# Background matmuls in four column tiles, a lead-in that walks both head pairs by key chunk, and Q of the last two query chunks made later

## The chip, the cores and the metric

The kernel runs on one core of one Trainium2 chip. The metric is the device time of one execution in microseconds (us), taken from runs of the changed kernel and of the kernel before that alternate on the same chip. The time before was 1268.96 us (median of 3 runs). All comparisons are between fast runs.

The engines are called as in the profile. PE is TensorE (PEld its weight loads), DVE is VectorE, ACT is ScalarE, POOL is GpSimd, SP issues the DMAs. "L593" is line 593 of the kernel that the view belongs to.

## The reference

One pre-LN transformer block in bf16, with sequence 2048, width 1024, 32 heads of 32, and an FFN of width 3584.

```python
def _A_ref(x, wqkv, wo):                       # attention, no mask
    q, k, v = split(x @ wqkv)                  # H = 32 heads, Dh = 32
    p = softmax(einsum("bhqd,bhkd->bhqk", q, k) * Dh ** -0.5)
    return merge(einsum("bhqk,bhkd->bhqd", p, v)) @ wo
def _B_ref(x, w1, b1, w2, b2):
    return gelu(x @ w1 + b1) @ w2 + b2         # tanh form
h  = x + _A_ref(_layernorm(x), wqkv, wo)
h2 = h + _B_ref(_layernorm(h), w1, b1, w2, b2)
```

## The kernel before

The kernel states every operation as a task with an estimated cost. A list scheduler written in Python then fixes the instruction order of each engine before the kernel is built. On the chip each engine is given its list in that order and waits on semaphores.

The 2048 queries are four chunks of 512. Attention goes over chunks, then over 16 head pairs, then over 16 key tiles, so there are 1024 exponentials of 128x1024 on ACT, 256 to a chunk. "qk" matmuls use the PE array in four row tiles, "pv" matmuls (with the softmax sum) in four column tiles. Four such matmuls, one for each tile, are issued as a pack. Everything else on the PE is "background" (bg): the Q, K and V projections while chunk 0 runs, and the output projection Wo, the second layer norm's transposes and the FFN of chunk n-1 while chunk n runs. Background has one PSUM bank (7), pv has one (6), qk has six.

```python
def proj(which, g, tc, bank, evac, direct=False):      # Q or K of head group g (two pairs), 512 tokens
    for dc in range(DC):
        pe(lambda p, dc=dc: p.matmul(psum[:, bank, :], Wall[:, blk, dc, c:c + P], xnT[:, tc, dc, :], ...),
           MM, ...)                                     # mode="full" by default
    ...                                                 # copy to stg; K: 4 copies into KT2; Q: to DRAM
def layer_norm(x_ap, B_x, o_ap, B_o, prio):             # one tile of 128 tokens
    ...                                                 # DVE: statistics; POOL: 7 tiny steps
    dve(lambda v: v.tensor_scalar(o_ap, x_ap, mvr[:, i, :], rden[:, i, :], ALU.subtract, ALU.mult), ...)
...
for tc in range(4):                                     # the lead-in: one key chunk after another
    for t4 in range(4):
        ...; ln_tile(tt, xslot[tt], 0)
        tr_tile(tt, xslot[tt], lb(), "act")             # 8 transposes, copied out by ACT
    proj(1, 0, tc, lb(), "act")
    ...
    attention_round(0, 0, 2 * tc)                       # pair 0 only
    for t4 in range(4): proj_v(4 * tc + t4, 0, lb(), "act")
    attention_round(0, 0, 2 * tc + 1)
def rest_of_projections():
    for g in range(1, G):
        for tc in range(4): proj(1, g, tc, 7, "dve")
        proj(0, g, 0, 7, "dve")
        ...                                             # V of the other 512 columns while g is 1..3
    for tc in range(1, 4):                              # Q of chunks 1, 2, 3
        for g in range(G): proj(0, g, tc, 7, "dve")
...
for qc in range(1, NCH):
    wo_ln2(R1, qc - 1, [7]); ffn1(R1, qc - 1, [7]); ffn2(R1, qc - 1, [7])
    attention_chunk(qc); attention_flush()
```

When a head pair is done, `finish` copies the pv bank to `Osb` and `Dsb`. After every second pair it takes reciprocals and writes `OT[g]`. `Osb`, `Dsb` and `OT` exist once: `OT[g]` can't be written while Wo of the previous chunk still reads it, and until it is written the next pair can't empty the pv bank.

The softmax here doesn't subtract the row's maximum and nothing guards it: scores larger than these inputs give would overflow.

## Time and profile before

| stretch | what | measured |
|---|---|---|
| 0 to 29 us | x, layer norm, first K, Q | first exponential at 29.2 |
| 29 to 331 | chunk 0, with all of K, Q, V | 302 us for 256 exponentials |
| 332 to 1119 | chunks 1, 2, 3 | 261, 262, 262 us |
| 1119 to 1267.5 | tail: Wo, layer norm, FFN of chunk 3, full-width matmuls | 149 us |

Exponentials were counted in the trace's records. A chunk goes from the start of its first to the start of its last exponential. Without any wait a head pair of 16 takes 14.8 us, and 256 exponentials take 237 us.

The page's first part gives busy time, share of the span and instructions by engine:

```profile
PE 1156.2 (91%) x9099; PEld 377.0 (30%) x9248; DVE 676.7 (53%) x1148; ACT 1052.7 (83%) x1174; POOL 67.3 (5%) x236
```

The stretches view has, per stretch, busy us and (instructions) of PE, PEld, DVE, ACT, POOL, then clock, DMA share and GB/s:

```profile
100.00:200.00 100.00, 92.56 (x754) 29.32 (x771) 44.29 (x94) 85.17 (x93) 0.00 (x0) 1.00 0.10 30
...
500.00:600.00 100.00, 92.20 (x782) 24.21 (x794) 27.39 (x38) 97.85 (x103) 0.00 (x0) 1.00 0.17 56
```

ACT is nearly full from about 300 us on, and the PE is at 92% beside it. In the first 300 us ACT has room. The timeline of ACT (start us, duration us, instruction, count, and in brackets the wait before it) shows one whole gap:

```profile
76.25 15.49 ACT L593 ACTIVATE PT<-ps 128x1024 bf16<-128x1024 f32 x16
102.52 27.82 ACT L593 ACTIVATE PT<-ps 128x1024 bf16<-128x1024 f32 x30 [10.77 <-PE ps L583]
```

The timeline of the PE in a steady round shows what fills the PE (L719 background, L583 qk, L603 one half of a pv pack; the other half, L607, is left out):

```profile
602.00 0.39 PE L603 MATMUL ps<-PT,V 128*32 128x512 bf16 x2
...
602.23 0.38 PE L603 MATMUL ps<-PT,V 128*32 128x512 bf16 x2
...
602.55 0.39 PE L719 MATMUL ps<-a_w2r,gT 128*128 128x512 bf16 x1
...
602.87 0.40 PE L583 MATMUL ps<-QT_67,KT_65 32*128 32x512 bf16 x4
...
603.20 0.82 PE L719 MATMUL ps<-a_w2r,gT 128*128 128x512 bf16 x3
...
603.95 0.39 PE L603 MATMUL ps<-PT,V 128*32 128x512 bf16 x2
```

Read the starts: two pv packs are 0.23 us apart, but pv to background takes 0.32, background to qk 0.32, and qk to background 0.33. Each change of array mode adds about 0.1 us. The trace has 1731 changes.

### The profile page before, as it was taken

To read this page: it belongs to the slowest core of one execution; us is meant where nothing else is said; L and a number is where in the kernel's file an instruction comes from. 1 tells how busy PE (TensorE), PEld (TensorE's weight loads), DVE (VectorE), ACT (ScalarE), POOL (GpSimd) and SP (SyncE) were. 2 spreads that over 40 slices of the span, in tenths; PEclk is the share of its full clock that TensorE was granted. 3 is DMA by queue.
4 is the path that set the end of the run, shared out by engine and by line. 5 is a ranking of instruction groups with operands and counts; after the bars stand their busy time and mean duration, and the time that the engine had idled before them with its cause. 6 is when DMAs were issued, how large, how long until landed. Compare 5 with 4: busy or idle time off the path is not lost.

```text
span 1267.5 us, 21571 instructions
## 1 busy us (share of the span) xinstructions
PE 1156.2 (91%) x9099; PEld 377.0 (30%) x9248; DVE 676.7 (53%) x1148; ACT 1052.7 (83%) x1174; POOL 67.3 (5%) x236
## 2 busy tenths in 40 slices
PE   5999998999998999999989999999899999996989
PEld 2432222233322232222232332222323322233434
DVE  4534446543447886222368882222689832237971
ACT  3777877999999999999999999999999999930220
POOL 5500000000011000000020000000200000002000
PEclk9999999999999999999999999999999999997989
DMA  5740020021132322040523320404433303041404
GB/s 141 167 116 13 13 76 17 26 88 47 43 92 80 87 81 63 18 133 18 168 75 88 88 72 18 134 18 138 125 88 94 107 22 110 25 146 50 117 10 140
DMA packets 152098, 99.84 MB, mean 79 GB/s; under 512 B 25153, under 2 KB 149953, under 8 KB 152002
## 3 DMA queue, kind: packets, MB, share of 16 engines
q1 hardware_dynamic: 152002, 98.47, 26.7%
q8 instruction: 72, 1.18, 0.4%
q14 instruction: 24, 0.20, 0.0%
HBM read 89.92 MB, written 8.26 MB: 77 GB/s over the span
## 4 chain that ended last, share of the span: by engine, by line
PE 67%; DVE 20%; ACT 5%; issue 4%; POOL 3%; DMA 1%; SPq 0%; POOLq 0%; DVEq 0%
PE ps L719 16%; PE ps L603 16%; PE ps L583 10%; PE ps L511 9%; PE ps L685 8%; ACT PT L593 4%; PE ps L660 3%; PE ps L552 3%; DVE a_xh L690 3%; DVE gT L698 2%; DVE Osb L617 2%; DVE Dsb L621 2%; DVE a_uu L694 2%; DVE Dsb L615 2%; DVE st L461 1%
## 5 line engine op out<-in xcount | busy, mean ns | idle before, releaser
L593 ACT ACTIVATE PT<-ps 128x1024 bf16<-128x1024 f32 x1024 | 969.3, 1034 | 51.6 <-PE ps L583 40.4
L603 PE MATMUL ps<-PT,V 128*32 128x512 bf16 x2048 | 312.7, 384 | 25.7 <-DVE Osb L617 21.1
L607 PE MATMUL ps<-PT,ones_50 128*32 128x512 bf16 x2048 | 312.6, 385 | 0.0
L719 PE MATMUL ps<-a_w2r,gT 128*128 128x512 bf16 x848 | 239.8, 387 | 5.4 <-issue 4.9
L583 PE MATMUL ps<-QT_67,KT_65 32*128 32x512 bf16 x2048 | 202.3, 385 | 12.4 <-ACT PT L593 8.4
L685 PE MATMUL ps<-hnT,a_w1r 128*128 128x512 bf16 x630 | 166.8, 382 | 14.1 <-DVE a_xh L690 7.1
L615 DVE COPY Dsb<-ps 64x512 f32<-64x512 f32 x64 | 44.4, 693 | 250.1 <-PE ps L607 248.2
L511 PE MATMUL ps<-xnT,Wall 128*128 128x512 bf16 x478 | 128.3, 387 | 8.0 <-DVE stg L520 3.8
L603 PEld LDWEIGHTS ps<-PT,V 128*32 128x32 bf16 x2048 | 67.6, 94 | 202.8 <-issue 148.4
L621 DVE RECIPROCAL Dsb<-Dsb 128x128 f32<-128x128 f32 x128 | 113.7, 924 | 0.5
L583 PEld LDWEIGHTS ps<-QT_67,KT_65 32*128 32x128 bf16 x2048 | 52.0, 91 | 198.6 <-ACT PT L593 149.0
L719 PEld LDWEIGHTS ps<-a_w2r,gT 128*128 128x128 bf16 x896 | 69.3, 98 | 138.4 <-issue 98.4
L520 DVE CAST stg<-ps 128x512 bf16<-128x512 f32 x59 | 40.3, 683 | 106.7 <-PE ps L511 92.6
L696 ACT ACTIVATE b_th<-b_uu 128x512 f32<-128x512 bf16 x28 | 17.6, 630 | 88.0 <-DVE b_uu L694 88.0
L685 PEld LDWEIGHTS ps<-hnT,a_w1r 128*128 128x128 bf16 x672 | 53.8, 97 | 100.1 <-issue 33.7
L690 DVE TENSOR_SCALAR a_xh<-ps,b1f 128x512 bf16<-128x512 f32 x84 | 62.2, 741 | 22.5 <-PE ps L685 20.6
L552 PE MATMUL ps<-Wall,xnT 128*128 128x512 bf16 x245 | 61.3, 381 | 9.6 <-DVE V L559 4.5
L511 PEld LDWEIGHTS ps<-xnT,Wall 128*128 128x128 bf16 x512 | 44.2, 98 | 85.6 <-issue 29.8
L607 PEld LDWEIGHTS ps<-PT,ones_50 128*32 128x32 bf16 x2048 | 67.5, 94 | 0.0
L660 PE MATMUL ps<-a_w1r,OT 128*128 128x512 bf16 x256 | 65.7, 382 | 0.1
L698 DVE SCALAR_TENSOR_TENSOR gT<-a_th,a_xh 128x512 bf16<-128x512 f32 x84 | 56.7, 675 | 16.2 <-ACT a_th L696 15.9
L464 POOL CAST mvb<-mv 128x2 bf16<-128x2 f32 x32 | 7.2, 230 | 1077.1 <-DVE mv L463 1077.1
(53 smaller groups left out, 706.7 us busy)
## 6 DMA issues: line engine op xcount, KB each, us to landing
a_w2r<-in_B_w_dram SPq DMA_DIRECT2D x56, 512.0 KB, 4.5
a_w1r<-in_B_w_dram SPq DMA_DIRECT2D x42, 512.0 KB, 3.9
a_w1r<-in_A_wo_dram SPq DMA_DIRECT2D x16, 512.0 KB, 3.8
QT_67<-q_scratch SPq DMA_DIRECT2D x62, 128.0 KB, 2.7
b_w1r<-in_B_w_dram SPq DMA_DIRECT2D x14, 512.0 KB, 3.8
Wall<-in_A_wqkv_dram SPq DMA_DIRECT2D x16, 256.0 KB, 5.2
xr<-in_A_x_dram SPq DMA_DIRECT2D x16, 256.0 KB, 2.9
a_xr_82<-in_A_x_dram SPq DMA_DIRECT2D x32, 128.0 KB, 3.3
```

The costliest lines, as they stand in the source:

```text
L511: pe(lambda p, dc=dc: p.matmul(psum[:, bank, :], Wall[:, blk, dc, c:c + P], xnT[:, tc, dc, :], start=(dc == 0), stop=(dc == DC - 1)), MM, ...
L552: pe(lambda p, dc=dc: p.matmul(psum[:, bank, :], xnT[:, tc, dc, t4 * P:(t4 + 1) * P], Wall[:, blk, dc, :], start=(dc == 0), stop=(dc == DC ...
L583: return p.matmul(psum[:, 2 * us[half] + j, :], KT2[r0:r0 + 32, p16, tc, i, :], QT2[r0:r0 + 32, qs, pr, :], start=True, stop=True, tile_po ...
L593: act(lambda a, u=u, s=s: a.activation(PT[:, s, :, :], psum[:, 2 * u:2 * u + 2, :], ACT.Exp, bias=0.0, scale=SCALE), 1024, reads=[B_ps[2 * ...
L603: fns.append(lambda p, j=j, h=h: p.matmul(psum[32 * j:32 * j + 32, 6, :], V[:, kt, 32 * h:32 * h + 32], PT[:, s, j, :], start=first, stop= ...
L607: fns.append(lambda p, j=j: p.matmul(psum[64 + 32 * j:96 + 32 * j, 6, :], ones32[:, :], PT[:, s, j, :], start=first, stop=last, tile_posit ...
L621: dve(lambda v, k=k: v.reciprocal(Dsb[:, 128 * k:128 * k + 128], Dsb[:, 128 * k:128 * k + 128]), 0.9, reads=[B_Dsb[0][k], B_Dsb[1][k]], wr ...
L660: pe(lambda p, g=g, k=k, s=s, t4=t4, bank=bank: p.matmul(psum[:, bank, :], OT[:, g, t4 * P:(t4 + 1) * P], R.w1[:, s:s + 2, g, :], start=(k ...
L685: pe(lambda p, dc=dc, s=s, f=f, bank=bank: p.matmul(psum[:, bank, :], R.w1[:, s, dc, f * P:(f + 1) * P], hnT[:, dc, :], start=(dc == 0), s ...
L690: dve(lambda v, i=i, fc=fc, bank=bank: v.tensor_scalar(R.xh[:, i, :], psum[:, bank, :], b1f[:, fc:fc + 1], None, ALU.add), c_dve_ps(512), ...
L698: dve(lambda v, i=i, fc=fc: v.scalar_tensor_tensor(gT[:, fc, :], R.th[:, i, :], 1.0, R.xh[:, i, :], ALU.add, ALU.mult), c_dve(512), reads= ...
L719: pe(lambda p, fc=fc, s=s, t4=t4, bank=bank: p.matmul(psum[:, bank, :], gT[:, fc, t4 * P:(t4 + 1) * P], R.w2[:, s, fc % 4, :], start=False ...
```

## The change

The change has three intents. Background matmuls become four column tiles of 32, so that they share pv's mode. The lead-in does both pairs of g=0 per key chunk, with only a quarter of V, so that exponentials start earlier and denser. Q of chunks 2 and 3 leaves the crowded chunk 0. One part of the second intent is easily read over: for key chunks 1 to 3 the last step of the layer norm moves from DVE to POOL, planned at 1.4 us a tile.

```diff
+    def mm(bank, lhsT, rhs, start, stop, reads, narrow, cols=(0, 512)):
...
+        if narrow:                                     # all background but the tail's
+            for j in range(4):
+                fns.append(lambda p, j=j: p.matmul(psum[32*j:32*j+32, bank, c0:c1], lhsT[:, 32*j:32*j+32], rhs,
+                           start=start, stop=stop, tile_position=(0, 32 * j), skip_group_check=True))
+            pe(fns, occ, ..., mode="col")
...
+    def layer_norm(tiles, prio, norm="dve"):           # up to four tiles share the small steps
+            eng, cost = (dve, 0.58) if norm == "dve" else (pool, 1.4)
+            eng(lambda e, ...: e.tensor_scalar(o_ap, x_ap, mvr[...], rden[...], ALU.subtract, ALU.mult), cost, ...)
...
+    def late_q(R, qc):                                 # Q of chunk qc from x kept in DRAM, weights through the FFN ring
...
     for tc in range(4):
+        ev = "act" if tc == 0 else "dve"
+        for h in ((0, 1), (2, 3)) if tc == 0 else ((0, 1, 2, 3),):
+            ln_tiles([tts[k] for k in h], 0, "dve" if tc == 0 else "pool")
...
+        for k in range(8):
+            att.qk(0, [(k % 2, 4 * tc + k // 2)])      # both pairs, one key tile each
+            if k == 1: proj_v(4 * tc, 0, lb(), ev)     # 256 columns of V, two token tiles
+            if k == 3: proj_v(4 * tc + 2, 0, lb(), ev)
...
     for qc in range(1, NCH):
+        if qc + 1 < NCH:
+            late_q(R1, qc + 1)
         wo_ln2(R1, qc - 1, [7])
```

Also changed: 20 warm-up matmuls at the start, other costs in the scheduler, one more PT buffer, and `PV_FORCE` (how many pv packs may wait before the scheduler puts them ahead of background) raised from 3 to 5.

## The prediction

> **What bounds it now.** The timeline of the scalar engine shows three stretches. (1) Lead-in and first query chunk: the first exponential starts at 29.2 us, the 256 of chunk 0 end at 331. Dense exponentials start every 0.92 us (14.8 us for one head pair of 16), so 256 need 237 us: about 65 us are lost, 10.8 us of it in one gap at 92 to 102 us, where the PE finishes K and Q of the next pair. (2) Chunks 1 to 3: 261 us each, against 254 us of scalar work (237 + 28 tanh of about 0.6). The stretches table has ACT 97 to 98% busy, PE 92 to 94%; both are nearly full. (3) A tail from the last exponential (1119 us) to the end, 148 us, PE work at full width.
>
> In a steady round of 1.95 us the timeline shows one bg matmul, qk, three bg, two pv, bg again: four changes of array mode. Starts are 216 ns apart between bg matmuls but 309 from bg to pv, 321 back, 327 after qk: each change costs about 0.1 us. I count 1731 changes, some 170 us of PE time. The Trainium skill ("TensorEngine Tiling (Array Packing)", Key Properties) says a change of tiling mode drains the array; this trace agrees, at 0.1 us.
>
> **What the change does.**
> - Background matmuls in four column tiles share pv's mode, so a round has two changes: about 700 fewer, 70 us of PE time. Packs of four pv matmuls follow each other in 216 to 227 ns, so I cost a column-tiled 512-column matmul at 0.2225 us, and a 256-column piece at 0.115, an estimate from the same spacing. It quadruples the instructions (eight per pack). No pv run here is longer than five packs, so sustained issue is unproven; the 256-column V pieces are the worst. The same page says column tiling disables Fast Weight Load; pv's four loads took 0.1 us, hidden.
> - Lead-in: 32 exponentials instead of 16, V only a quarter at first, evictions moved from ACT to DVE. Per key chunk I estimate PE 13 us, DVE 12, ACT 8, against 14.3 us now. Warm-up matmuls and earlier x loads bring the first exponential to about 26 us. But both pairs of g=0 are spent when the lead-in ends (about 74 us), and K and Q of g=1 (13.5 us on one bank, then 7 us through DRAM) are exposed: a gap of 12 to 20 us, next exponential about 94 us (102 now).
> - Chunk 0 afterwards: per g, 72 matmul-equivalents (16 us) plus attention 14 us = 30 us, against 29.6 us of ACT: balanced. It ends near 306 us: -25 us.
> - Chunks 1 and 2 get 64 matmuls of Q each: PE about 244 of 254 us. Late Q delays Wo, which holds the output tiles and so may stall pv for some us. I take 258, 257, 255: -13 us.
> - Tail: fewer POOL steps in layer norm, -2 us; with the backlog gone the PE idles 6 us before Wo. Net about 0.
>
> Sum: 1269 - 25 - 13 - 2 = 1229 us.
>
> **What would show it.** Steps between column packs near 220 ns; about 1050 changes; exponentials of pair 2 from about 94 us; chunk 0's last near 306 us; chunks 1 to 3 at 255 to 258 us; last exponential near 1080 us; tail unchanged at 146 to 149 us.
>
> **What would make it wrong.** Column packs issue-bound (over 0.25 us, V pieces over 0.15): chunk 0 stays PE-bound and the gain shrinks to 1 or 2%. A longer gap after the lead-in, or pv stalls behind Wo. On the other side, a faster lead-in, or chunk 0 wholly ACT-bound: near 1210 us.
>
> Chances: faster 0.75, same 0.21, slower 0.04. Range 1205 to 1256 us.

## The result, and the profile after

The changed kernel took 1264.05 us (median of 4 runs, 1263.26 to 1266.15) against 1269.44 (4 runs). The ratio is 0.9958, with a 95% interval of 0.994 to 0.9975. Ratios are the mean time of one kernel's fast runs over that of the other's of the same rounds, so not quite the ratio of the medians. The change gained 0.4%, where 3.2% was forecast.

| | before | after | predicted |
|---|---|---|---|
| first exponential, us | 29.2 | 25.5 | 26 |
| period of a key chunk in the lead-in, start to start | 12.9 to 14.4 | 22.8 to 23.8 | about 13 to 14 |
| first exponential of pair 2 | 102.5 | 130.3 | 94 |
| last exponential of chunk 0 | 331 | 342.6 | 306 |
| chunks 1, 2, 3 | 261, 262, 262 | 255.5, 260.6, 254.2 | 258, 257, 255 |
| start of the last exponential to the end | 149.5 | 145.8 | unchanged |
| mode changes | 1731 | 1086 | 1050 |

Page, first part, then two stretches of the lead-in and the two that answer to those shown of before:

```profile
PE 1154.2 (91%) x17266; PEld 465.2 (37%) x17276; DVE 686.6 (54%) x1186; ACT 1027.8 (81%) x1145; POOL 83.6 (7%) x108
```

```profile
40.00:60.00 20.00, 14.77 (x230) 7.47 (x230) 9.45 (x22) 7.76 (x8) 12.81 (x8) 0.76 0.14 41
60.00:80.00 20.00, 13.79 (x226) 7.29 (x222) 8.04 (x18) 6.74 (x7) 13.84 (x8) 0.76 1.06 210
100.00:200.00 100.00, 90.98 (x1798) 43.70 (x1800) 50.85 (x110) 71.86 (x77) 0.00 (x0) 0.97 0.12 35
...
500.00:600.00 100.00, 99.01 (x1608) 37.69 (x1604) 27.08 (x37) 99.70 (x109) 0.00 (x0) 1.00 0.35 102
```

From 500 to 600 us ACT is now 99.7% busy, where it was 97.9%. That is what the column tiles were for. In the two lead-in stretches shown, no engine is busy more than three quarters of the time (PE 69 to 74%, POOL 64 to 69%), and the clock is down to 0.76. The PE timeline of a steady stretch shows that the tiles themselves did what was hoped (L435 is now all narrow background; x4 is one pack):

```profile
523.63 0.38 PE L649 MATMUL ps<-PT,V 128*32 128x512 bf16 x2
...
523.84 0.82 PE L435 MATMUL ps<-a_w2r,gT 128*32 128x512 bf16 x12
524.60 0.39 PE L629 MATMUL ps<-QT_65,KT_63 32*128 32x512 bf16 x4
524.92 0.40 PE L435 MATMUL ps<-a_w2r,gT 128*32 128x512 bf16 x4
525.15 0.38 PE L649 MATMUL ps<-PT,V 128*32 128x512 bf16 x2
```

Between pv and background a start now follows after 0.21 to 0.23 us, in either direction. Over the whole trace a pack of four takes 216 ns, and a 256-column V pack 109 ns (medians). So neither the quadrupled instructions nor the weight loads cost anything that shows here.

The loss is in the lead-in. The ACT timeline shows waits between the key chunks, and then a long one:

```profile
60.63 1.02 ACT L638 ACTIVATE PT<-ps 128x1024 bf16<-128x1024 f32 x1 [0.70 <-PE ps L629]
72.05 4.69 ACT L638 ACTIVATE PT<-ps 128x1024 bf16<-128x1024 f32 x5 [10.38 <-PE ps L629]
...
95.52 7.69 ACT L638 ACTIVATE PT<-ps 128x1024 bf16<-128x1024 f32 x8 [8.28 <-PE ps L629]
...
130.34 1.94 ACT L638 ACTIVATE PT<-ps 128x1024 bf16<-128x1024 f32 x2 [27.14 <-PE ps L629]
```

The wait is put down to the qk matmuls on the PE, but the PE was itself waiting. The waits view for 20 to 103 us says for what (us in total, times, longest):

```profile
PE ps L504 <- POOL xb L498: 22.3, 12, 2.7
```

L504 are the transposes, and L498 is the last step of the layer norm, now on POOL. The POOL timeline of one key chunk, with the start of the next:

```profile
47.31 0.19 POOL L488 CAST mvb<-mv 128x8 bf16<-128x8 f32 x1 [6.76 <-DVE mv L485]
...
49.03 1.01 POOL L494 TENSOR_TENSOR rden<-denb,cexp 128x4 f32<-128x4 bf16 x1
50.21 15.07 POOL L498 TENSOR_SCALAR xb<-xrb,mvr,rden 128x1024 bf16<-128x1024 bf16 x4 [0.18 <-DVE st L483]
71.09 0.19 POOL L488 CAST mvb<-mv 128x8 bf16<-128x8 f32 x1 [5.80 <-DVE mv L485]
```

From 47.31 to 71.09 is the period of 23.8 us: 2.9 us of small steps, 15.1 us for four tiles, and 5.8 us in which POOL waits for DVE statistics. The groups view gives the mean of the same step, in ns, before and after (the number just before the second bar):

```profile
L474 DVE TENSOR_SCALAR xb<-xr,mvr,rden 128x1024 bf16<-128x1024 bf16 x16 | 8.6, 542 | 10.1 <-POOL rden L472 10.0
```

```profile
L498 POOL TENSOR_SCALAR xb<-xrb,mvr,rden 128x1024 bf16<-128x1024 bf16 x8 | 30.2, 3782 | 0.4 <-POOL rden L494 0.2 <-DVE st L483 0.2
```

The step takes 542 ns on DVE and 3782 ns on POOL, 7.0 times as long. All twelve on POOL took 3.78 to 3.79 us, whatever the DVE was doing beside them. The diff plans it at 1.4 us. The Trainium skill ("GPSIMD Engine Reference", sections 3.1 and 4.1) says that two-input elementwise work there is about two times slower than on VectorE, and one-input work about at line rate. For this step, with one tensor input and two per-partition scalars, the trace doesn't agree, and the measurement decides.

### The profile page after: what moved, and what is told of

Read it like the earlier page. It is cut to its first block, busy times and chain, and to the rows that moved or that the text cites. A ratio compares the mean times of both kernels' runs of the same rounds, so it can differ in the third digit from the quotient of the medians.

```text
span 1261.5 us, 37733 instructions
## 1 busy us (share of the span) xinstructions
PE 1154.2 (91%) x17266; PEld 465.2 (37%) x17276; DVE 686.6 (54%) x1186; ACT 1027.8 (81%) x1145; POOL 83.6 (7%) x108
## 3 DMA queue, kind: packets, MB, share of 16 engines
q1 hardware_dynamic: 162978, 106.85, 29.2%
## 4 chain that ended last, share of the span: by engine, by line
PE 57%; ACT 27%; DVE 10%; POOL 4%; issue 2%; DMA 0%; POOLq 0%; DVEq 0%
PE ps L435 30%; ACT PT L638 26%; PE ps L439 9%; PE ps L649 9%; PE ps L629 8%; POOL xb L498 4%; DVE a_xh L728 3%; DVE gT L736 1%; DVE stg L544 1%; DVE Dsb L667 1%; DVE a_uu L732 1%; PE ps L504 1%; DVE Osb L663 1%; DVE st L483 1%; DVE Dsb L661 1%
## 5 line engine op out<-in xcount | busy, mean ns | idle before, releaser
L435 PE MATMUL ps<-hnT,a_w1r 128*32 128x512 bf16 x3200 | 211.2, 382 | 14.9 <-DVE a_xh L728 13.9
L435 PE MATMUL ps<-a_w2r,gT 128*32 128x512 bf16 x2688 | 196.5, 381 | 0.0
L649 PEld LDWEIGHTS ps<-PT,V 128*32 128x32 bf16 x2048 | 96.8, 97 | 125.3 <-issue 36.0
L661 DVE COPY Dsb<-ps 64x512 f32<-64x512 f32 x64 | 44.4, 694 | 131.1 <-PE ps L653 129.8
L435 PE MATMUL ps<-xnT,Wall 128*32 128x512 bf16 x1536 | 107.4, 400 | 8.3 <-DVE stg L544 6.1
L435 PEld LDWEIGHTS ps<-hnT,a_w1r 128*32 128x32 bf16 x3200 | 72.6, 96 | 114.4 <-issue 38.5
L435 PEld LDWEIGHTS ps<-a_w2r,gT 128*32 128x32 bf16 x2688 | 68.5, 96 | 81.9 <-issue 28.3
L653 PEld LDWEIGHTS ps<-PT,ones_50 128*32 128x32 bf16 x2048 | 96.8, 97 | 0.0
L734 ACT ACTIVATE b_th<-b_uu 128x512 f32<-128x512 bf16 x28 | 17.6, 630 | 84.2 <-DVE b_uu L732 84.2
L435 PE MATMUL ps<-Wall,xnT 128*32 128x256 bf16 x2048 | 67.3, 274 | 3.3 <-DVE V L602 2.4
L758 DVE SCALAR_TENSOR_TENSOR a_ost<-ps,hch 128x512 bf16<-128x512 f32 x24 | 16.4, 684 | 97.0 <-PE ps L435 96.9
L544 DVE CAST stg<-ps 128x512 bf16<-128x512 f32 x46 | 31.2, 678 | 55.7 <-PE ps L435 55.6
L435 PEld LDWEIGHTS ps<-xnT,Wall 128*32 128x32 bf16 x1536 | 37.4, 100 | 61.7 <-issue 20.6
```

What stands on the lines that cost most here:

```text
L435: fns.append(lambda p, j=j: p.matmul(psum[32 * j:32 * j + 32, bank, c0:c1], lhsT[:, 32 * j:32 * j + 32], rhs, start=start, stop=stop, tile ...
L544: dve(lambda v: v.tensor_copy(stg[:, s, :], psum[:, bank, :]), c_dve_ps(512), reads=[B_ps[bank]], writes=[B_stg[s]])
L649: fns.append(lambda p, j=j, h=h: p.matmul(psum[32 * j:32 * j + 32, bank, :], V[:, kt, 32 * h:32 * h + 32], PT[:, s, j, :], start=first, st ...
L653: fns.append(lambda p, j=j: p.matmul(psum[64 + 32 * j:96 + 32 * j, bank, :], ones32[:, :], PT[:, s, j, :], start=first, stop=last, tile_po ...
L661: dve(lambda v: v.tensor_copy(Dsb[64 * pr:64 * pr + 64, :], psum[64:128, bank, :]), c_dve_ps(512), reads=[B_ps[bank]], writes=B_Dsb[pr], p ...
```

## The experiments

Theory A: the norm on POOL paces the lead-in. Rival B: the column packs, the V pieces or the slow clock do. Rival C: POOL's time would be hidden, were it not for a fixed order made from a wrong cost. Other theories came later, as below. Times are medians of the fast runs; the ratio is to before. The kernel before was near 1269 us.

| run | edit, on top of | time, us | ratio [95%] |
|---|---|---|---|
| e1 | norm on DVE, on after | 1240.6 | 0.9767 [0.9747, 0.9787] |
| e2 | POOL planned at 3.8 us, on after | 1251.4 | 0.9868 [0.9842, 0.9895] |
| e3 | background at full width, on after | 1303.2 | 1.026 [1.0232, 1.0288] |
| e4 | column tiles alone, on before | 1248.3 | 0.9837 [0.982, 0.9854] |
| e5 | e1 again | 1240.5 | 0.9768 [0.9745, 0.979] |
| e6 | K, Q of g=1 in the lead-in, on e1 | 1237.2 | 0.9743 [0.9719, 0.9766] |
| e7 | late Q after the first FFN part, on e1 | 1227.9 | 0.9672 [0.9649, 0.9695] |
| e8 | e6 and e7, norm on ACT | 1230.0 | 0.9688 [0.9662, 0.9714] |
| e9 | Q of g=1 before K, on e7 | 1235.1 | 0.9722 [0.9704, 0.974] |
| e10 | dummy matmuls in the tail, on e7 | 1224.9 | 0.9649 [0.9626, 0.9672] |
| e11 | no late Q, on e7 | 1243.7 | 0.9793 [0.9773, 0.9814] |
| e12 | lead-in walks one pair, on e7 | 1228.7 | 0.9671 [0.9651, 0.9692] |
| e13 | late Q moved as in e7, on after | 1265.3 | 0.9965 [0.9934, 0.9997] |
| e14 | late Q moved, on e2 | 1248.3 | 0.9825 [0.9797, 0.9852] |
| e15 | e7 again | 1230.4 | 0.9686 [0.966, 0.9712] |
| e16 | e10 again | 1225.5 | 0.9646 [0.9621, 0.9671] |

All sixteen gave correct results.

### e1 and e5: the norm on DVE

```diff
-            ln_tiles([tts[k] for k in h], 0, "dve" if tc == 0 else "pool")
+            ln_tiles([tts[k] for k in h], 0, "dve")
```

> The changed kernel with one word changed: the layer norm's last step (subtract mean, times reciprocal) of key chunks 1 to 3 runs on the vector engine instead of POOL. In the changed kernel's trace this step takes 3.78 us per tile on POOL (0.54 on DVE), four tiles per key chunk, 15.1 us of a 23.8 us key-chunk period. Theory A (POOL paces the lead-in): the period falls to about 15 us, the exponentials of pair 2 start near 102 us instead of 130, the time falls by about 25 to 28 us to 1237 us. Rival B (the column-tiled matmuls or their 256-column V pieces pace the lead-in, or the half-rate PE clock there does, and the POOL wait is only slack): the period stays above 20 us and the time within 8 us of 1264.

> The same kernel as e1_norm_dve, run again only because that run's profile fell in a slow state (clock 0.65, 1608 us) and can't be read. Expected time 1240 us as its fast runs were. Theory A: key-chunk period of about 15 us, no POOL wait before the transposes; exponentials of pair 2 from 100 to 105 us after a gap of 20 to 27 us in which K and Q of g=1 are made; chunk 2 again 260 us or more, with a stall in its fourth pair.

Theory A holds, and rival B falls: with every pack and piece left in place, exponentials come in clean groups of eight, 12.6 to 13.9 us apart. ACT timeline of e5:

```profile
36.55 7.44 ACT L638 ACTIVATE PT<-ps 128x1024 bf16<-128x1024 f32 x8 [4.07 <-PE ps L629]
...
63.04 7.69 ACT L638 ACTIVATE PT<-ps 128x1024 bf16<-128x1024 f32 x8 [6.05 <-PE ps L629]
94.27 18.30 ACT L638 ACTIVATE PT<-ps 128x1024 bf16<-128x1024 f32 x19 [23.54 <-PE ps L629]
```

Pair 2 starts at 94.3 us (after: 130.3; I had expected 100 to 105) and chunk 0 ends at 307.1 (after: 342.6), 35 us sooner. But the time fell by only 24 us. Chunks 1, 2 and 3 took 256.4, 271.0 and 256.7, and nearly all of the growth in chunk 2 is in its fourth pair, 29.6 us (after: 19.6). Some of the gain had turned into a new wait; e7 takes that up. The clock theory needs no run of its own. The stretches view of the lead-in, first of the changed kernel and then of e5, has the clock at 0.73 and at 0.98, though only the norm moved, so the slow clock followed from the norm on POOL:

```profile
25.00:100.00 75.00, 52.04 (x748) 25.69 (x744) 24.85 (x53) 28.47 (x30) 50.45 (x21) 0.73 0.56 140
25.00:100.00 75.00, 64.23 (x1240) 34.66 (x1240) 46.93 (x101) 35.70 (x40) 5.09 (x9) 0.98 0.56 144
```

### e2: the same work, planned with its true cost

```diff
-            eng, cost = (dve, 0.58) if norm == "dve" else (pool, 1.4)
+            eng, cost = (dve, 0.58) if norm == "dve" else (pool, 3.8)
```

> The changed kernel with the norm left on POOL, but the kernel's own scheduler told that it costs 3.8 us instead of 1.4, so that the fixed order of every engine is planned with the true duration. Theory A (the POOL work itself): the lead-in keeps a period of 20 us or more, time 1255 to 1264 us. Rival C (the wrong cost only made a bad static order: the work in POOL would be hidden in the right order): the period falls under 17 us and the time under 1245 us.

This came out between the two theories. POOL no longer waits for DVE: its period is 17.9 us, with no idle time marked before the first step of a key chunk (POOL timeline of e2):

```profile
40.03 0.19 POOL L488 CAST mvb<-mv 128x8 bf16<-128x8 f32 x1
...
57.96 0.19 POOL L488 CAST mvb<-mv 128x8 bf16<-128x8 f32 x1
```

Pair 2 starts at 110.5 us, and the time is 1251 us. So the wrong plan had a large part of the loss, and POOL's duration the rest. Chunk 2 grew here too (266.8 us, fourth pair 26.8), so the share of each is not to be read from this run. e13 to e15 below do that.

### e3 and e4: the column tiles, taken out and alone

```diff
-        if narrow:
+        if False:                        # e3, on the changed kernel
```

In e4 the four-tile `mm` replaces the background matmuls of the kernel before, and nothing else changes.

> The changed kernel with the background matmuls at full width again (one 128-column matmul instead of four column tiles), lead-in and everything else as changed. Measures the column tiles alone. If they save what the fewer mode changes promise (about 700 fewer at 0.1 us of PE time each, of which some 30 us in the stretches where the PE is the limit), the time rises by 15 to 35 us to about 1280 to 1300 us, chunks 1 to 3 take 262 us or more instead of 254 to 261. If the tiles give nothing: within 5 us of 1264.

> The kernel before with nothing but the background matmuls made as four column tiles (tail at full width as in the changed kernel); lead-in, Q and layer norm as before. Measures the column tiles in the other setting. Theory A (the change's loss lies in the lead-in, its tiles gain): mode changes fall from 1731 to about 1100, chunks 1 to 3 take 254 to 257 us instead of 261, chunk 0 gains 10 to 20 us, time about 1240 us (1230 to 1250), that is, faster than the whole change. Rival D (the tiles' quadrupled instructions cost about what the drains cost): within 6 us of 1269.

e4: 1056 changes of mode, chunks 258, 256, 256, chunk 0 298, and 21 us gained in all. The sum of the three chunks is 770 us, as in the changed kernel (770), against 784 before. Rival D (the instructions cost what the drains cost) falls. My 10 to 20 us for chunk 0 did not come: it gained 3. The column tiles alone beat the whole change, which tells that the rest of the change lost 16 us. e3 lost 39 us, more than I allowed; the fourth pairs of chunks 1 and 2 took 29 and 32 us. The tiles are thus worth 21 us in one setting and 39 in the other. In the second, the slower background also delayed Wo (see e7).

### e7, e11: what late Q does to Wo

```diff
-        if qc + 1 < NCH:
-            late_q(R1, qc + 1)
         wo_ln2(R1, qc - 1, [7])
         ffn1(R1, qc - 1, [7])
+        if qc + 1 < NCH:
+            late_q(R1, qc + 1)
         ffn2(R1, qc - 1, [7])
```

> Norm on the vector engine as in e1, and the late Q of the next query chunk put after the first FFN matmuls instead of ahead of Wo. In the changed kernel the fourth pair of chunk 2 took 19.6 us against 16.5 in chunk 3, which has no late Q; in e2 26.8. Theory G (late Q ahead of Wo holds the output tiles, so the fixed output and denominator buffers and the one pv bank wait): the fourth pair of chunk 2 falls to 16 to 17 us, chunk 2 to 254 to 256 us, time 4 to 10 us under 1240. Rival: the stall has another cause, and stays.

First the stall in e5. DVE timeline (L669 writes `OT`, L661 and L663 then empty the pv bank), with the ACT wait of 600 to 665 us in the waits view:

```profile
627.29 0.64 DVE L669 TENSOR_TENSOR OT<-Osb,Dsb 128x512 bf16<-128x512 f32 x1
...
629.11 0.69 DVE L661 COPY Dsb<-ps 64x512 f32<-64x512 f32 x1
629.81 0.68 DVE L663 COPY Osb<-ps 64x512 f32<-64x512 f32 x1
```

```profile
ACT PT L638 <- PE ps L653: 11.8, 1, 11.8
```

Wo's last matmul started at 622.8 us, 57 us after the chunk began. Only then could `OT` be written, the pv bank emptied, pv go on, and the exponentials find buffers. (`OT` came another 4 us later: DVE had layer norm work ahead of it in the fixed order.) In the changed kernel Wo's last matmul came 53 us after the chunk's start, and the same wait was 3.6 us. In e7 it came after 44 us, and the wait is:

```profile
ACT PT L638 <- PE ps L653: 2.5, 1, 2.5
```

Theory G holds. Chunk 2 fell from 271.0 to 258.7 (I had said 254 to 256; its fourth pair still took 19.1), and the time by 12.6 us to 1227.9.

> e7 with Q of query chunks 2 and 3 made in chunk 0 again, as in the kernel before (no late Q). 128 matmuls of 0.216 us move back, 28 us of PE time. If chunk 0 is bound by the PE: chunk 0 ends 20 to 28 us later, chunks 1 and 2 gain at most 5 us together, time 1245 to 1255 us. If chunk 0 is bound by ACT: time within 5 us of 1228.

In e11 Q of chunks 2 and 3 is again made ahead of the other background. I expected chunk 0 to grow by 20 to 28 us. It ended at 306.0 us, where e7's ended at 306.3. The extra matmuls simply ran on into chunk 1, ahead of Wo, and chunk 1 took 276 us (258), with a fourth pair of 34.8 us. So late Q does gain (16 us), not by freeing the PE in chunk 0, as I had put it, but by keeping Q out of Wo's way. The changed kernel then put it in Wo's way in chunks 1 and 2.

### e6, e8, e9: the gap at the end of the lead-in

In e6 `proj(1, 1, tc)` goes into each key chunk, and Q of g=1 goes straight to its place. In e8 the same is joined with e7, with the norm as an ACT `Identity` with scale and bias. In e9 Q of g=1 is projected before its K, with K on two banks.

> Norm on the vector engine as in e1, and in addition K of g=1 made key chunk by key chunk inside the lead-in, Q of g=1 in its second key chunk and moved straight into place without the trip through DRAM. Theory E (after POOL is repaired, what the lead-in still loses is the exposed K and Q of g=1, because both pairs of g=0 are spent): the gap of 20 to 27 us before pair 2 shrinks to under 6 us, each key chunk grows by 1 to 3 us, time 1222 to 1230 us against 1240. Rival F (the PE is the limit of chunk 0 anyway, so the work only moves): within 5 us of 1240.

> Both e6 and e7, and the norm of key chunks 1 to 3 on the scalar engine, which has idle time in the lead-in (about 8 of 15 us), instead of the vector engine. A candidate for the best version. If the repairs add and the vector engine paces the lead-in of e6 (its sum is about 16 us per key chunk): time 1212 to 1222 us. If not, about the sum of e6 and e7: 1218 to 1226 us.

> e7 with one more edit: for g=1, Q is projected before K instead of after, and its K groups alternate two PSUM banks, so that Q's trip through DRAM runs under the K matmuls. In e7 the exponentials stand still for 22.8 us at the end of the lead-in. Theory H (the gap is that chain: four K groups, Q, then DRAM): the gap falls to 10 to 14 us. What it is worth: if chunk 0 is bound by ACT after the gap, all of it, 9 to 12 us, time 1216 to 1219 us; if the PE, 97 to 99% busy in that stretch, is the limit, most of it comes back as slower pairs and the time falls by 0 to 5 us.

The gap is real (23.5 us in e5), but none of three ways to close it made chunk 0 end sooner: 309.2 us in e6, 307.8 in e8 and 311.7 in e9, against 307.1 in e5 and 306.3 in e7. e6 is still 3 us faster than e5, because its chunks 2 and 3 took 266.8 and 254.5 us and not 271.0 and 256.7. It had a fault of its own: the copy of Q queued behind five weight transfers, and the staging slot waited for it 5.5 us. It gives no verdict on the gap. In e8 the gap before pair 2 fell from 22.8 to 0.9 us, but key chunks took 17.6 to 19.8 us and the next two pairs 18.3 and 18.1. e9 was 7 us slower than e7, and its gap was still 20.6 us, where I had expected 10 to 14: both pairs of g=0 end together, and their finish on DVE stood in front of the copy that the PE waited for. Timeline of e9:

```profile
81.89 3.39 DVE L667 RECIPROCAL Dsb<-Dsb 128x128 f32<-128x128 f32 x4
...
86.66 3.60 PE L435 MATMUL ps<-xnT,Wall 128*32 128x512 bf16 x32 [8.80 <-DVE stg L544]
```

What sets the end of chunk 0 near 306 us in e5, e7, e8 and e12 alike was argued, not shown. I take it to be the PE work due before g=2 can start: what is made early for g=1 is missing for g=2. e11 rules out the sum of all PE work in chunk 0.

### e12: one pair or both

```diff
-        for k in range(8):
-            att.qk(0, [(k % 2, 4 * tc + k // 2)])
-            ...
+        for k in range(2):
+            attention_round(0, 0, 2 * tc + k)
+            proj_v(4 * tc + 2 * k, 0, lb(), ev)
```

> e7 with the lead-in walking one head pair, in rounds of two key tiles as in the kernel before, and the second pair of g=0 following after it, over K and Q of g=1. It tells what walking both pairs brings once POOL is out of the way. Theory I (chunk 0 is bound by the PE's sum, so the order of the two pairs matters little): within 5 us of 1228, the gap before pair 2 mostly gone but the lead-in emptier. Rival (the walk itself is a gain): 8 us or more above 1228.

1228.7 us against 1227.9 of e7, with the same ratio. Walking both pairs brings nothing: pair 1 fills the lead-in but is then missing to cover K and Q of g=1. Theory I's outcome holds (its reason, the PE's sum, is what e11 put in doubt).

### e10, e16: the tail's clock

> e7 with dummy matmuls where the PE waits in the tail: 24 after the last pv matmul, 28 after the last Wo matmul. The clock records of e7 show the PE at half clock for 13.7 us from 1079.6 and again from 1106.9. If the PE's idle times cause that and it costs time in Wo and in the first FFN matmuls: both half-clock stretches go or shrink under 4 us, tail 4 to 7 us shorter, time 1221 to 1224 us. If the layer norm chain on the other engines sets the tail: within 2 us of 1228.

> The same kernel as e10. If the dummy matmuls help: 2 to 4 us under e15. If e10's lead was another chip: within 1 us of e15.

On one chip, e16 took 1225.5 us (1223.5 to 1228.3) and e15 1230.4 (1229.6 to 1231.3). No run of one lies among those of the other, but the intervals of the ratios overlap a little, and e10 against e7 gave 3 us on two chips, so I call it 3 to 5 us. The first profile is of e7, the second of e10; both show Wo and the first matmuls of the FFN:

```profile
1087.77 16.68 PE L439 MATMUL ps<-a_w1r,OT 128*128 128x512 bf16 x64 [5.73 <-DVE OT L669]
...
1115.97 50.58 PE L439 MATMUL ps<-hnT,b_w1r 128*128 128x512 bf16 x219 [1.19 <-DVE hnT L510]
```

```profile
1087.75 13.98 PE L439 MATMUL ps<-a_w1r,OT 128*128 128x512 bf16 x64
...
1113.09 48.52 PE L439 MATMUL ps<-hnT,b_w1r 128*128 128x512 bf16 x224 [0.93 <-DVE hnT L510]
```

Wo is 2.7 us shorter. In e7 its first 5.5 us fell in a half-clock stretch (1079.6 to 1093.3 us), which accounts for that. In e10 the stretch still begins, but ends at 1085 us, before Wo, and the next one comes only at 1167 us. I had expected 4 to 7 us from e10 and 2 to 4 from e16; 3 and 5 were measured. That the layer norm chain sets the rest of the tail is argued, not shown. e10 (e16) is the best version I ran: 0.965 of before.

### e13, e14: the shares

> The changed kernel with the late Q behind the first FFN matmuls, norm left on POOL at its wrong planned cost. If the two losses simply add (12 us for the stall as in e7 against e5): about 1252 us. If the stall mattered little while POOL held the lead-in back (the scalar engine waited 3.6 us there in the changed kernel, 11.8 in e5): 1257 to 1262 us.

> As e13, but with the POOL norm planned at 3.8 us. Against e15 (norm on the vector engine) it holds the duration of the POOL norm alone. In e2 the exponentials of pair 2 began at 110.5 us, in e5 at 94.3: so the POOL duration should cost 14 to 18 us, time 1241 to 1246 us. If POOL's duration were harmless once planned: within 5 us of e15.

> The same kernel as e7, on the chip of e16: about 1228 us, 0.967 of before.

With the late Q out of Wo's way in all three, they differ in the norm alone: on POOL and planned at 1.4 us 1265.3, on POOL and planned at 3.8 us 1248.3, on DVE 1230.4. So, repaired in this order, the wrong plan costs 17 us and the POOL duration 18 us, 35 in all; the ends of chunk 0 (341.6, 324.6 and 306.8 us) differ by the same 17 and 18. And e13 is no faster than the changed kernel (1264.05), which neither of my two figures had: chunk 2 fell from 260.6 to 256.7 us, but chunks 1 and 3 and the tail took as much back. The two losses don't add; the second costs time only when the first is repaired.

## Why the prediction was wrong

The prediction was 1229 us (1205 to 1256), the result 1264.

- Right: what bound the kernel before (mode changes of 0.1 us, ACT and PE both near full); column packs at 0.2225 us (measured 0.216) and V pieces at 0.115 (0.109); 1050 changes (1086); the first exponential at 26 us (25.5); chunks 1 and 3 at 258 and 255 (255.5 and 254.2). That the three chunks together gained 14 us, where 13 were forecast, is in part luck: with the lead-in on time, as the forecast had it (e5), they took 784.0 us and gained nothing, until late Q was moved (e7).
- The step that failed: "Per key chunk I estimate PE 13 us, DVE 12, ACT 8, against 14.3 us now." The sum left POOL out, though the diff moves the norm of three key chunks there. POOL takes 18 us per key chunk (2.9 + 15.1), more than any engine in the list, and with the order planned for 1.4 us a tile the period was 23.8 us. With it went "the lead-in ends (about 74 us)" (measured: about 103 us), "next exponential about 94 us" (130.3) and "It ends near 306 us" (342.6). With the norm on DVE (e5) the last two are 94.3 and 307.1, so the rest of that chain was sound. Chunk 0 ended 36.6 us late, which is the whole error of the forecast, and e13 against e15 puts the norm's cost at 35 us. That these agree does not mean that the norm alone was wrong: with only the norm repaired the change takes 1240.5 us, still 11 above the forecast, and that is the late-Q step below.
- The gap of "12 to 20 us" after the lead-in was mis-sized: 27 us after, 23.5 with POOL repaired. I had left out that both pairs finish on DVE just then, ahead of the copies of K and Q that the PE waits for (5.8 us of such waits in e5). How the rest divides is not shown.
- "Late Q delays Wo, which holds the output tiles and so may stall pv for some us" was the right mechanism, at 3.6 us in the result. Its size was wrong as soon as the lead-in was on time: 11.8 us of wait in e5, and 271.0 us for chunk 2 against my 257 (260.6 in the result). In e5 the background was further behind: Wo of chunk 2 began 31.2 us into the chunk, in the changed kernel 25.8.
- "Tail: ... Net about 0." It gained 3.7 us (149.5 to 145.8), although Wo ran partly at half clock (1110 to 1127 us in the clock record).
- My list of what could go wrong named issue-bound packs first. They were not. "A longer gap after the lead-in, or pv stalls behind Wo" was there, without a cause on POOL.

## What to carry to other kernels

Sum a stage over every engine, and above all over the engine to which the change moves work: here an operation of 0.54 us on one engine cost seven times as much on another, and because the order is planned ahead from costs, the wrong cost lost as much again. Read one duration of the moved operation from a chip before trusting its cost. After a repair, look for the wait it uncovers: here a single-buffered output held by late readers took back a third of the gain (12 of 36 us) until the work queued ahead of those readers was moved.

## What the Trainium skill lacked or had wrong

- "GPSIMD Engine Reference", sections 3.1 and 4.1: two-input elementwise work about 2 times slower than VectorE (its measured pair is an fp32 `tensor_tensor`), one-input work about at line rate. A bf16 `tensor_scalar` with two operations and per-partition scalars over 128x1024 took 3782 ns on POOL (x12) and 542 ns on DVE, 7.0 times.
- "TensorEngine Tiling (Array Packing)", Key Properties: a mode change drains the array, without a figure. Here it costs about 0.1 us between full width, four row tiles and four column tiles, in any direction.
- The same page, Restrictions: column tiling disables Fast Weight Load. A full-width 512-column matmul split into four column tiles still took 216 ns per pack, as much as the undivided one, and a 256-column one 109 ns. The loads were hidden.
- "TensorE: Matmul & The Clock Gate", Part 1: half clock after at least one idle window of about 3.4 us. Half-clock stretches in the fast traces here last 3.41, 6.83, 10.24, 13.65 or 17.07 us, which agrees with the window. But in the 3.41 us before the one that began at 1078 us in e10, some matmul started at least every 0.91 us, and the PE was busy for 62% of the time. Before the four that began in or just after the changed kernel's lead-in (31.0, 54.9, 78.8 and 109.5 us) a matmul started at least every 2.8 us, with the PE busy for 23 to 37%. So the clock fell without a whole idle window. The same part does say, under "A second HAM failure mode", that short idles between groups of matmuls make the clock swing; the table alone would mislead.
- The same part names clock ratios K/N of 4/8, 8/8, for several busy cores 13/16 (0.81), and a stuck 1/4. The slow run of e1, a program on one core, has 0.65 in its clock record for most of 1608 us, which no page explains.
